# A linear-attention and feed-forward kernel: batch 1 in the nine-token layout, and the first part of q as fp32 by SyncE

## The chip, the cores and the metric

One core of one Trainium2 chip. The metric is the device time of a run in microseconds (us); every figure of a run is a median of the runs named beside it. The **granted clock** is the share of its full clock that the throttle gave TensorE, as the profile records it. A profile is of one execution. Its span is about 1.7 us shorter than the device time of the same run (295.1 against 296.85 for the kernel before).

## The reference

```python
# q, k, v: (8 batches, 8 heads, 576 tokens, 64), fp32
def phi(x):
    return np.where(x > 0, x, np.exp(x) - 1.0) + 1.0
q_p, k_p = phi(q), phi(k)
kv  = np.einsum('bhsd,bhse->bhde', k_p, v)
z   = np.sum(k_p, axis=2)
num = np.einsum('bhsd,bhde->bhse', q_p, kv)
den = np.einsum('bhsd,bhd->bhs', q_p, z)[..., None] + 1e-06
x   = (num / den) -> (4608 tokens, 512)
h   = x @ w_in                                   # 512 x 2048
g   = h * (1.0 / (1.0 + np.exp(-beta * h)))      # beta: 2048 numbers
out = g @ w_out                                  # 2048 x 512
```

The kernel computes phi as min(relu(x) + 1, exp(x)), and takes beta into ScalarE's Silu and 1/beta into w_out.

## The kernel before

Batch 0 stands in a **nine-token layout**: heads 0 to 3 on partitions 0 to 63, heads 4 to 7 on partitions 64 to 127, nine tokens on each partition (64 x 9 = 576). The other batches have four tokens on each of 128 partitions and a **tail** of 64 tokens on the first 64 partitions, whose other half has to be cleared. The parts that matter here:

```python
def load_rows(dst, src, b, eng=nc.gpsimd):       # four tokens per partition, and the tail
    eng.dma_start(out=dst[:, :, 0:NJ, :]...,     in_=src[b, :, 0:MAIN, :]...)   # 128 partitions
    eng.dma_start(out=dst[0:TAIL, :, NJ, :],     in_=src[b, :, MAIN:S, :]...)   # 64 partitions

def load_nine(dst, src, h0=0, h1=HH, j0=0, j1=N9):    # nine tokens: one load for each half
    for g in range(2):
        nc.gpsimd.dma_start(out=dst[g * TAIL : (g + 1) * TAIL, h0:h1, j0:j1, :]..., in_=...)
...
small = consts.tile([P, 2], F32)
nc.vector.memset(small, 0.0)
nc.scalar.activation(small[:, 0:1], small[:, 0:1], ACTF.Exp)
nc.vector.memset(g_sb[0][:, FC - 1, :], 0.0)     # operand of the warm-up matmuls
clear_tail(1); nc.vector.memset(vraw[1][TAIL:P, :, NJ, :], 0.0)
nc.sync.dma_start(out=beta_row, in_=moe_beta.rearrange("(c p) -> c p", p=P))
load_nine(k9, k)
load_nine(q9, q, j1=4)
load_nine(v9, v, j1=6); load_nine(v9, v, j0=6); load_nine(q9, q, j0=4)
for i in range(4): ...                           # w_in, four quarters, by GpSimd
load_w_out(0); load_w_out(1); load_k(1); load_q(1)
...                                              # the front
warm(10)                                         # ten warm-up matmuls
beta_trans(); make_beta()                        # TensorE transposes beta, VectorE works on it
warm(20)                                         # twenty more
exp0(1, 0, 5); exp0(1, 5, N9); exp0(0, 0, 4)     # k first, q's first four tokens last
relu0(1, 0, 5); relu0(1, 5, N9); phi0(1, 0, 5)
relu0(0, 0, 4); phi0(1, 5, N9); phi0(0, 0, 4)
kv_mm0(kvp, 0, N9, False)                        # z
... q transposes, v's part of kv, numerator, x, feed-forward part of batch 0
load_w_out(2); load_v(1); load_w_out(3)
...                                              # batch 1's attention, inside batch 0's y matmuls
y_phase_wide(0, {
    4: [load_next(3)],
    9: [kv_mm(1), kv_evac(1), w_out_scale(3)],
    10: [q_trans(1, 0, 1), q_trans(1, 2, 3)],
    11: [num_mm(1, 0), num_norm(1, 0)], ...
```

In these traces each engine takes its instructions in the order of the program, so a matmul that waits also holds those written behind it (twenty stood behind one that waited 3.52 us in the changed kernel). Names in the profile: `xqk` and `vraw` hold the loaded q, k and v, `vaug` is v copied beside columns of ones, `qk_p` is phi(q) and phi(k), `kv_bd` the evacuated kv, `xs` a block of x, `g` the output of Silu (and at the start the buffer of q's fp32 part).

## Time and profile before

| | before |
|---|---|
| time, median of 3 runs (lowest to highest) | 296.29 us (296.06 to 296.74) |
| span of the profiled run, granted clock | 295.1 us, 1.000 |
| TensorE busy | 283.9 us, 96% |
| beta: issued, then landed after | 0.75 us, 1.5 us |
| first feed-forward matmul | 17.16 us |
| first matmul of batch 0's second product (y) | 34.16 us |
| v of batch 1 landed; its kv matmuls start | 41.84 us; 43.23 us |
| first feed-forward matmul of batch 1 | 52.53 us |

The lines behind this stand in the prediction below. In a line of the timeline the first two numbers are start and duration in us; then engine, source line, operation, output and inputs, and in brackets the idle time of the engine before it and what ended that time. Four **anchors** on TensorE are used throughout: first feed-forward matmul, first y matmul, kv matmuls of batch 1, first feed-forward matmul of batch 1.

### The profile page before, as it was taken

The page shows a single profiled execution, that of the slowest core. Times are in us where ns is not written, and L with a number is a line of the kernel's source. Part 1 is how long each engine was busy: PE and PEld are TensorE (multiplying, and loading weights), DVE is VectorE, ACT ScalarE, POOL GpSimd, SP SyncE. Part 2 cuts the span into 40 slices and gives each one's busy share as a digit, 9 for nine tenths or more (in the row PEclk, how much of TensorE's full clock was granted, in tenths as well). Part 3 has the DMA queues.
Part 4 walks back from the last instruction along what each step waited for, and adds up shares of the span by engine and source line. Part 5 has one row for each costly group of instructions (what it writes and reads, how often), then busy time and mean ns, then how long its engine had stood idle before and what let it go on. Part 6 is the DMA issues. An engine that isn't in the chain of part 4 may idle for free.

```text
span 295.1 us, 4750 instructions
## 1 busy us (share of the span) xinstructions
PE 283.9 (96%) x1891; PEld 143.9 (49%) x1912; DVE 124.0 (42%) x261; ACT 175.1 (59%) x234; POOL 52.7 (18%) x72
## 2 busy tenths in 40 slices
PE   8879999999999999999999999999999999999994
PEld 3557445644465544445444544454445444444444
DVE  4765488504365174616461646154715400110012
ACT  2788786889988780778087907790770077018500
POOL 8924474540003200330023000000000000000000
PEclk9999999999999999999999999999999999999999
DMA  7999999999637993699369945024502400120032
GB/s 103 196 207 343 256 272 192 256 193 192 89 142 100 175 131 113 130 174 154 98 129 159 159 109 124 2 71 116 127 0 72 118 36 0 38 90 16 0 73 71
DMA packets 72310, 37.09 MB, mean 126 GB/s; under 512 B 40912, under 2 KB 66784, under 8 KB 72288
## 3 DMA queue, kind: packets, MB, share of 16 engines
q0 software_dynamic: 38912, 20.45, 47.9%
q1 hardware_dynamic: 33216, 16.20, 22.9%
q8 instruction: 15, 0.25, 0.3%
q10 hardware_dynamic: 160, 0.13, 0.2%
q14 instruction: 7, 0.06, 0.1%
HBM read 36.71 MB, written 9.44 MB: 156 GB/s over the span
## 4 chain that ended last, share of the span: by engine, by line
PE 76%; DMA 9%; POOL 4%; ACT 4%; issue 4%; DVE 1%; ACTq 0%; POOLq 0%; DVEq 0%
PE mm L453 37%; PE mm L505 33%; DMA xT<-in_moe_w_out_dram 5%; DMA vraw<-in_v_dram 4%; PE att L399 3%; ACT e L229 2%; POOL xqk L131 1%; PE att L344 1%; PE mm L537 1%; POOL w_in L159 1%; ACT L229 1%; POOL vraw L131 1%; ACT g L445 1%; DVE qk_p L242 0%; POOL xqk L111 0%
## 5 line engine op out<-in xcount | busy, mean ns | idle before, releaser
L445 ACT ACTIVATE g<-mm,beta_c 128x512 bf16<-128x512 f32 (+2 forms) x156 | 97.3, 633 | 88.4 <-PE mm L453 88.1
L505 PE MATMUL mm<-w_out,g 128*128 128x512 bf16 x541 | 126.7, 379 | 1.2 <-issue 0.3
L453 PE MATMUL mm<-xT,w_in 128*128 128x512 bf16 (+2 forms) x560 | 108.1, 349 | 1.4 <-DMA w_in<-in_moe_w_in_dram 1.1
L453 PEld LDWEIGHTS <-w_in 128*128 128x128 bf16 x656 | 61.9, 98 | 62.4 <-DMA w_in<-in_moe_w_in_dram 1.2
L505 PEld LDWEIGHTS <-g 128*128 128x128 bf16 x560 | 53.0, 98 | 58.2
L515 DVE COPY y_sb<-mm 128x512 f32<-128x512 f32 x27 | 18.7, 691 | 70.6 <-PE mm L505 69.1
L229 ACT ACTIVATE e<-xqk 128x2560 bf16<-128x2560 bf16 x14 | 31.9, 2329 | 0.1
L415 DVE TENSOR_TENSOR xs<-att,rden 128x512 bf16<-128x512 f32 (+1 forms) x40 | 27.6, 689 | 1.4
L242 DVE TENSOR_TENSOR qk_p<-r,e 128x2560 bf16<-128x2560 bf16 x14 | 20.9, 1490 | 13.1 <-ACT e L229 12.4
L355 DVE CAST kv_bd<-att 64x130 bf16<-64x130 f32 x28 | 8.2, 292 | 32.2 <-PE att L344 31.8
L72 POOL DMA_DIRECT2D vraw<-in_v_dram x7 | 6.4, 909 | 84.2 <-DVE vaug L370 78.5
L413 DVE TENSOR_SCALAR den<-att 128x8 f32<-128x8 f32 (+1 forms) x40 | 6.5, 161 | 32.0 <-PE att L399 31.9
L399 PE MATMUL att<-kv_bd,q_pT 128*128 128x130 bf16 (+1 forms) x160 | 15.8, 221 | 1.1 <-DVE kv_bd L370 0.7
L399 PEld LDWEIGHTS <-q_pT 128*128 128x128 bf16 (+1 forms) x160 | 11.6, 100 | 10.7 <-DVE xs L415 2.4
L453 PE MATMUL mm<-xT_tail,w_in 128*128 128x512 bf16 x63 | 13.9, 379 | 0.1
L237 DVE TENSOR_SCALAR r<-xqk 128x2560 bf16<-128x2560 bf16 x14 | 11.6, 834 | 3.8 <-DMA xqk<-in_q_dram 2.3
L575 PE MATMUL mm<-g 128*128 128x512 bf16 x34 | 9.9, 452 | 1.2 <-DVE g L143 1.2
L229 ACT ACT_TABLE_LOAD x7 | 9.0, 1283 | 0.1
L414 DVE RECIPROCAL rden<-den 128x8 f32<-128x8 f32 (+1 forms) x40 | 8.1, 202 | 1.4
L72 POOL DMA_DIRECT2D xqk<-in_k_dram x7 | 6.9, 984 | 6.3 <-DMA w_in<-in_moe_w_in_dram 2.8
L76 POOL DMA_DIRECT2D xqk<-in_k_dram x7 | 7.4, 1057 | 1.5 <-DMA w_in<-in_moe_w_in_dram 1.3
L256 ACT ACTIVATE e<-xqk 128x1280 bf16<-128x1280 bf16 (+1 forms) x4 | 4.4, 1155 | 5.4 <-DMA xqk<-in_k_dram 5.3
(71 smaller groups left out, 140.0 us busy)
## 6 DMA issues: line engine op xcount, KB each, us to landing
out_dram<-y_sb SPq DMA_DIRECT2D x28, 256.0 KB, 2.3
xqk<-in_k_dram POOLq DMA_DIRECT2D x7, 512.0 KB, 10.7
xqk<-in_q_dram POOLq DMA_DIRECT2D x7, 512.0 KB, 11.3
vraw<-in_v_dram POOLq DMA_DIRECT2D x7, 512.0 KB, 11.3
w_in<-in_moe_w_in_dram POOLq DMA_DIRECT2D x4, 512.0 KB, 11.0
g<-in_moe_w_out_dram POOLq DMA_DIRECT2D x4, 512.0 KB, 10.9
out_dram<-y_sb SPq DMA_DIRECT2D x14, 128.0 KB, 5.2
xqk<-in_moe_w_out_dram POOLq DMA_DIRECT2D x2, 512.0 KB, 14.4
```

The source lines that it names most:

```text
L72: eng.dma_start(out=dst[:, :, 0:NJ, :].rearrange("p h j d -> p h (j d)"), in_=src[b, :, 0:MAIN, :].rearrange("h (p j) d -> p h (j d)", j=NJ),)
L229: nc.scalar.activation(st[b, "e", a][:, h0:h1], xqk[b % NX][:, a, h0:h1], ACTF.Exp)
L237: nc.vector.tensor_scalar(st[b, "r", a][:, h0:h1], xqk[b % NX][:, a, h0:h1], 0.0, 1.0, ALU.max, ALU.add)
L242: nc.vector.tensor_tensor(st[b, "p"][:, a].rearrange("p j (h d) -> p h j d", h=H)[:, h0:h1], st[b, "r", a][:, h0:h1], st[b, "e", a][:, h0: ...
L355: nc.vector.tensor_copy(kv_bd[b % 2][i][gs, :, g, :], st[b, "kvp"][gs, 2 * i : 2 * i + 2, :])
L399: nc.tensor.matmul(nps[:n, p // 2, c0 : c0 + 2 * (D + 1)], st[b, "qT"][:, t, p, :n], kv_bd[b % 2][p // 2][:, p % 2], start=True, stop=True ...
L415: nc.vector.tensor_mul(xs[:n], nv[:, :, :, 0:D], rden[:n, :, :, None].to_broadcast([n, 2, 4, D]))
L445: nc.scalar.activation(g_sb[b % 2][:, ff, c0:c1], hp[:, c0:c1], ACTF.Silu, scale=beta_c[:, ff : ff + 1],)
L453: nc.tensor.matmul(hp[:, c0:c1], w_in_sb[ff // 4][:, kc, (ff % 4) * P : (ff % 4 + 1) * P], x[:, t0:t1, kc, :] if b < B else x[:, kc, c0:c1 ...
L505: nc.tensor.matmul(yp, g_sb[b % 2][:, ff, t * P : (t + 1) * P], w_out_sb[ff // 4][:, ff % 4, :], start=(ff == 0), stop=(ff == FC - 1),)
L515: nc.vector.tensor_copy(y_sb, yp)
L575: nc.tensor.matmul(st["warm"], g_sb[0][:, FC - 1, 0:P], g_sb[0][:, FC - 1, :], start=True, stop=True, skip_group_check=True,)
```

## The change

Its intent: batch 1 takes the nine-token layout too, so that its tail loads, tail clearing and empty columns go. And the first four tokens of batch 0's q come through SyncE as fp32, while GpSimd issues the load of k, so that GpSimd's queue is shorter and idle DMA time at the start is used. The diff, cut to its core:

```diff
+    va9 = nine(vaug[1], "jhd", EA)
+    QF = 4
+    q_first = g_f[:, 0 : HH * QF * D].rearrange("p (h j d) -> p h j d", h=HH, j=QF)   # fp32
-    def load_nine(dst, src, h0=0, h1=HH, j0=0, j1=N9):
+    def load_nine(dst, src, b, j0=0, j1=N9, eng=nc.gpsimd):
 ...
-    clear_tail(1)
-    nc.vector.memset(vraw[1][TAIL:P, :, NJ, :], 0.0)
+    load_nine(q_first, q, 0, 0, QF, eng=nc.sync)
     nc.sync.dma_start(out=beta_row, in_=moe_beta.rearrange("(c p) -> c p", p=P))
-    load_nine(k9, k)
-    load_nine(q9, q, j1=4)
+    load_nine(x9[0][1], k, 0)
 ...
-    load_k(1)
-    load_q(1)
+    load_nine(x9[1][1], k, 1)
+    load_nine(x9[1][0], q, 1)
 ...                                   # the front: q's first part ahead of k
-    exp0(1, 0, 5) ... phi0(0, 0, 4)
+    exp9(0, 0, 0, QF); relu9(0, 0, 0, QF); phi9(0, 0, 0, QF)
+    exp9(0, 1, 0, 5); exp9(0, 1, 5, N9); relu9(0, 1, 0, 5); relu9(0, 1, 5, N9)
+    phi9(0, 1, 0, 5); phi9(0, 1, 5, N9)
 ...
-    load_v(1)
+    load_nine(v9[1], v, 1)
 ...                                   # batch 1
-    phi(1, 1); v_copy(1); phi(1, 0)
+    phi9(1, 1); v_copy9(); phi9(1, 0); tidy(1)        # tidy clears the tails for batch 4 and 3
+    def kv1():   36 matmuls of 130 columns, evacuation, ones for the later batches
+    def q1():    32 small transposes into one pair of banks, three copies by ScalarE
-        9: [F(kv_mm, 1), F(kv_evac, 1), F(w_out_scale, 3)],
-        10: [F(q_trans, 1, 0, 1, wide=True), F(q_trans, 1, 2, 3, wide=True)],
+        9: [F(kv1), F(w_out_scale, 3)],
+        10: [F(q1)],
```

Batch 1's rows of the output are stored as eight stores of 64 rows, not four of 128.

## The prediction

> **What bounds the kernel now.** I read the page first (busy shares, then the forty slices), then the chain of waits, then the waits of TensorE, then the timeline of the two stages that the change touches, and last the DMA's table in half-microsecond windows.
>
> ```profile
> PE 283.9 (96%) x1891; PEld 143.9 (49%) x1912; DVE 124.0 (42%) x261; ACT 175.1 (59%) x234; POOL 52.7 (18%) x72
> PE   8879999999999999999999999999999999999994
> DMA  7999999999637993699369945024502400120032
> PE 76%; DMA 9%; POOL 4%; ACT 4%; issue 4%; DVE 1%; ACTq 0%; POOLq 0%; DVEq 0%
> ```
>
> TensorE is busy 283.9 of 295.1 us, so everything that is not TensorE work comes to 11.2 us. The chain gives 76% to matmuls; its DMA and POOL pieces all lie before 42 us. The page's row of slices shows no hole after the third slice. A change that leaves the 541 + 560 large matmuls alone can only win from those 11.2 us, and from the small matmuls of batch 1. The first 1.2 us and the last 3 us are not touched.
>
> ```profile
> PE mm L453 <- DMA w_in<-in_moe_w_in_dram: 1.1, 1, 1.1
> PE att L399 <- DVE kv_bd L370: 0.7, 1, 0.7
> PE mm L433 <- DVE xs L415: 0.4, 1, 0.4
> PE mm L453 <- ACT xT L372: 0.3, 1, 0.3
> PE att L282 <- DVE qk_p L270: 0.3, 1, 0.3
> PE att L380 <- DVE kv_bd L355: 0.3, 1, 0.3
> PE att L344 <- DVE vaug L370: 0.3, 1, 0.3
> ```
>
> These are TensorE's waits up to 60 us. The first matmul of the feed-forward part waits 1.1 us for the first quarter of w_in. The waits on kv_bd (0.7), xs (0.4) and qk_p (0.3) belong to batch 0's attention; those on vaug and kv_bd (0.3 each, the last two lines) to batch 1's. The front, from the timeline:
>
> ```profile
> 7.49 3.16 ACT L256 ACTIVATE e<-xqk 128x1280 bf16<-128x1280 bf16 x3 [5.25 <-DMA xqk<-in_k_dram]
> 10.06 1.31 DVE L270 TENSOR_TENSOR qk_p<-r,e 128x1024 bf16<-128x1024 bf16 x2
> 11.68 1.19 PE L307 MATMUL mm<-vraw,qk_p 64*128 64x128 bf16 x36
> 15.88 0.42 DVE L370 COPY xT<-mm 128x512 bf16<-128x512 bf16 x1 [0.16 <-PE mm L433]
> 17.16 1.07 PE L453 MATMUL mm<-xT,w_in 128*128 128x128 bf16 x16 [1.10 <-DMA w_in<-in_moe_w_in_dram]
> ```
>
> k lands at 7.49, all of phi is ready at 11.37, the first block of x at 16.30, but w_in only at 17.1: the load ends last here, by 0.8 us. Batch 1's stage:
>
> ```profile
> 41.91 1.27 DVE L370 COPY vaug<-vraw 128x2560 bf16<-128x2560 bf16 x1 [0.69 <-DMA vraw<-in_v_dram]
> 43.10 1.47 DVE L242 TENSOR_TENSOR qk_p<-r,e 128x2560 bf16<-128x2560 bf16 x1
> 43.23 0.82 PE L344 MATMUL att<-vaug,qk_p 128*64 128x65 bf16 x40 [0.28 <-DVE vaug L370]
> 45.51 1.94 ACT L372 ACTIVATE q_pT<-att 128x1024 bf16<-128x1024 bf16 x2 [2.49 <-PE att L380]
> 40.00:50.00 10.00, 9.15 (x101) 5.25 (x101) 8.72 (x17) 6.14 (x8) 4.97 (x7) 1.00 1.44 243
> ```
>
> v lands at 41.84, VectorE copies it, then makes phi(q) and evacuates kv_bd, and TensorE (9.15 of 10 us busy) loses 0.85 us. VectorE at 8.72 of 10 is nearly full there.
>
> The DMA windows: columns after the five engines are clock, DMA share and GB/s, counted as bytes written, so a cast from fp32 reads twice that.
>
> ```profile
> 1.50:2.00 0.50, 0.50 (x2) 0.15 (x1) 0.50 (x2) 0.50 (x1) 0.50 (x2) 1.00 0.07 17
> 2.50:3.00 0.50, 0.50 (x3) 0.22 (x2) 0.50 (x2) 0.00 (x0) 0.50 (x2) 1.00 0.77 58
> 3.50:4.00 0.50, 0.50 (x3) 0.15 (x1) 0.28 (x4) 0.00 (x0) 0.50 (x2) 1.00 1.20 198
> ```
>
> From 3 us on the DMA is full: some 190 GB/s written, 380 read. Only before 2.5 us it is idle, but for beta's 8 KB, which SyncE issued at 0.75 and which moved before 2.0.
>
> **What the Trainium skill says.** "DMA: Bandwidth & Descriptors", section "Issuing engines are not separate DMA queues": loads issued by SyncE and by GpSimd run on the same 16 engines. So the new q load adds no bandwidth; it can win only what was idle. The trace agrees in that the total stays at one level, 180 to 210 GB/s written, from 3.5 to 22 us, however many loads are open. Same page, "SWDGE vs HWDGE vs iDMA": a cast in the load needs GpSimd. That is why this part of q comes as fp32. No run here shows the refusal. "TensorEngine Tiling (Array Packing)", section "Key Properties": row tiles work independently, and a change of tiling drains. The trace agrees on the first: 36 matmuls of 64 rows and 128 columns, 217 ns each, took 1.19 us, 33 ns from one to the next. "VectorE: DVE Perf Modes", section "Mode 2×_2P": an fp32 tensor_scalar can still make two results a cycle. The w_out scaling, 512 fp32 to bf16 in 0.48 us, is quicker than 512 cycles at the page's 0.96 GHz (0.53 us), so it agrees.
>
> **The change, part by part.**
>
> Start of the loads. 512 KB of q go out on SyncE at about 0.75 us, instead of 2 x 128 KB written by GpSimd behind k. By the beta load they move from about 1.6 us. At some 390 GB/s they need 1.35 us, of which 0.9 us lie before 2.5, in idle time; the other 0.45 us share with k. All GpSimd loads after k are also issued 1.26 us sooner (the two issues at 2.59 go). As the DMA is full, the landing of w_in moves by the idle time that was filled: 17.1 - 0.9 = 16.2 us. k loses the 0.45 us to the new load but no longer has q's pieces behind it; I expect it at 7.2 to 7.5, as before.
>
> Front arithmetic. VectorE starts on q after beta's small operations, which end at 7.03 as before (TensorE's ten warm-up matmuls gate them). Then: relu of 1024 fp32, estimated 0.75 (0.62 in bf16); phi(q) 0.68; two relus of k 1.15; phi(k) 0.83 + 0.68; together 4.1, gaps 0.15, so ready at 11.3, against 11.37 now. VectorE is the limit, not ScalarE, so doing q early wins nearly nothing here. But now k's phi comes last and not q's: behind it TensorE still has 16 z matmuls (about 0.25 us), then the 16 transposes and v's 36. End of these: 11.3 + 0.25 + 0.24 + 1.19 = 13.0, now 12.87. The rest of the front is unchanged: x ready at 16.4 instead of 16.3. With w_in at 16.2 the first matmul starts at 16.4, not 17.16: -0.75. The second block of x needs VectorE's second normalisation, ready at 17.34 now and 17.45 then; TensorE takes it up at 18.07 now, about 17.5 then. So I count 0.55 us from the front.
>
> Batch 1's loads. Each tensor now has two DMAs of 256 pieces of 2,304 B in place of 1,024 pieces of 1,024 B plus 512 of 256 B. From the landings (k, q and their tails end at 36.2, the w_out part before them at 29.9) a tensor of 1.18 MB takes 3.15 us; at 2,304 B I estimate the 400 GB/s at which w_in and w_out run, 2.9 us. Three tensors save 0.8 us. v then lands at 41.84 - 0.9 - 0.8 = 40.1. Its wait goes.
>
> Batch 1's arithmetic. exp, relu, phi and the copy of v run over 2,304 instead of 2,560 elements: a tenth less, that is 0.45 of 4.57 us on ScalarE, some 0.25 of 2.9 on VectorE for both phis. Then the 0.75 us of clearing tails (0.48 + 0.27) moves from the idle start into the full stretch of VectorE, ahead of the kv_bd evacuation. The kv matmuls become 36 of 130 columns in place of 40 of 65: 36 x 33 ns = 1.2 us against 0.82: +0.35. The q transposes become 32 + 4 small ones: at the 0.41 us of 16 in the front about 0.75 + 0.2, against 1.24 + 0.29: -0.55. The waits on vaug and on kv_bd go: -0.55. But the transposed q is now copied in three pieces, 0.6 + 0.6 + 1.02 us on ScalarE in place of 1.94, all from one pair of banks, and the second numerator needs that pair: I give back 0.3 us there, and 0.1 for mode changes. Net about -0.35, rounded down to -0.3 because VectorE is so full.
>
> Sum: -0.55 - 0.3 = -0.85 us. 296.29 - 0.85 = 295.4 us. The stores of batch 1 are eight of 64 rows in place of four of 128, far from the end: nothing.
>
> **The rivals.** First, the front takes all of it back: w_in early, but x late. For it speaks that VectorE has no slack between 7.03 and 11.4 and that k's matmuls now follow the last phi; if the fp32 load delays k by 0.8 us or more, or beta behind it lands after 5.6 us, x comes at 17.1 and the front gives nothing: 295.9 to 296.5. Against it: k's load no longer shares with the old q. Second, batch 1's stage turns from waiting for v to waiting for VectorE (tails and kv_bd) or for ScalarE's three copies: then its 0.3 is lost, and some 0.2 more: 295.7 to 296.0. The slice with 8.72 of 10 speaks for it; that the inputs are ready 1.7 us sooner speaks against it. Third, all waits go at once: front 0.8, batch 1 0.85 of idle time and 0.2 in matmuls: 294.4. The stretch from 65 to 83 us, where ScalarE's exponentials lead the chain, starts from TensorE's own results, so it should move along and neither eat nor add.
>
> **Range and chances.** The front may give 0 to 0.8, batch 1 from -0.2 to 1.0; the three runs of before spread over 0.7 us. I take 294.4 to 296.5 for 8 in 10. 2% is 5.9 us, more than half of all the time in which TensorE does not work, and no part of the change comes near it: faster 0.01, slower 0.01, within 0.98.
>
> **What would show it.** Right: the first feed-forward matmul at 16.2 to 16.7 with no wait, or a short one, on w_in; phi(k) last at 11.2 to 11.5; v landed near 40; no wait on vaug; kv matmuls of 1.1 to 1.3 us; small q transposes under 1 us in all; from 100 us on, the same timeline shifted by 0.5 to 1.2 us. Wrong: k after 8.2; TensorE waiting for beta; a new wait of over 0.4 us on the copies of transposed q or on kv_bd; or a shift that is there at 60 us and gone at 100.

## The result, and the profile after

The changed kernel takes 301.14 us (median of 4 runs, 300.49 to 301.47), the kernel before 296.43 in the same comparison (4 runs). The ratio is 1.0157, 95% interval 1.0135 to 1.0179. A ratio is always the mean time of one kernel's runs over that of the other's of the same rounds, so it is not quite the ratio of the medians. The kernel became 4.7 us slower: under 2%, but far outside the predicted range of 294.4 to 296.5, and in the other direction.

The page of the changed kernel (busy shares, two rows of the forty slices, the chain's shares):

```profile
PE 286.3 (96%) x1903; PEld 144.6 (48%) x1924; DVE 122.9 (41%) x262; ACT 174.8 (58%) x234; POOL 49.5 (17%) x70
PE   5889999999989999999999999999999999999994
PEclk9599999999999999999999999999999999999998
PE 86%; ACT 5%; issue 3%; DVE 2%; DMA 2%; SPq 0%; ACTq 0%
```

The span grew by 4.6 us (295.1 to 299.7), but TensorE is busy 2.4 us longer, with only twelve instructions more. The reason stands in the third line: in the second slice, from 7.5 to 15 us, the granted clock is 0.5. The first slice of TensorE fell from 8 to 5 tenths. So both new idle time and slower work lie in the first 15 us. DMA's share of the chain fell from 9% to 2%: the loads that led before no longer lead, because TensorE is later than they are. The start of that chain, in start and duration:

```profile
2.23 6.35 DMA beta_row<-in_moe_beta_dram
8.72 0.26 PE mm L191
8.97 7.32 PE mm L611 x20
16.29 0.54 PE mm L323 x36
```

Beta's 8 KB, issued at 2.23, needed 6.35 us. TensorE's transpose of beta (L191) waited for it, the twenty warm-up matmuls (L611) stand behind that in TensorE's order and took 7.3 us, and only then comes z (L323). It is the longest of TensorE's waits up to 60 us, and no wait on vaug or w_in is among them any more:

```profile
PE mm L191 <- DMA beta_row<-in_moe_beta_dram: 3.5, 1, 3.5
```

The busy times of the engines in two windows of the front (PE, PEld, DVE, ACT, POOL; then clock, DMA share, GB/s):

```profile
5.00:8.00 3.00, 0.19 (x1) 0.00 (x0) 0.00 (x0) 0.66 (x1) 2.91 (x5) 1.00 1.24 215
8.00:14.50 6.50, 5.78 (x15) 2.19 (x16) 4.84 (x11) 2.61 (x3) 5.23 (x7) 0.50 1.34 200
```

From 5.19 to 8.72 TensorE is idle. From 8.0 to 14.5 (14.8 in finer windows) it runs at half its clock. Beta costs VectorE the same idle time: its first beta operation waits 6.31 us for the transpose, though q has lain there since 7.3. The timeline of the front:

```profile
7.34 1.06 ACT L264 ACTIVATE e<-g 128x1024 bf16<-128x1024 f32 x1 [5.10 <-DMA g<-in_q_dram]
9.01 0.17 DVE L197 COPY beta_s<-mm 128x16 f32<-128x16 f32 x1 [6.31 <-PE mm L191]
10.21 0.88 DVE L272 TENSOR_SCALAR r<-g 128x1024 bf16<-128x1024 f32 x1
21.39 1.05 PE L487 MATMUL mm<-xT,w_in 128*128 128x128 bf16 x16 [0.29 <-DVE xT L404]
```

The first anchor moved from 17.16 to 21.39: +4.23 us. The second moved from 34.16 to 38.56, +4.40. Batch 1's stage:

```profile
44.77 0.97 DVE L358 COPY vaug<-vraw 128x2304 bf16<-128x2304 bf16 x1
47.29 1.21 PE L338 MATMUL att<-vaug,qk_p 64*128 64x130 bf16 x36
49.40 0.64 PE L291 MATMUL att<-identity,qk_p 64*128 64x64 bf16 x32
50.08 2.00 ACT L406 ACTIVATE q_pT<-att 128x512 bf16<-128x512 bf16 x3 [3.09 <-PE att L291]
57.01 0.60 PE L487 MATMUL mm<-xT,w_in 128*128 128x256 bf16 x4
```

No wait stands in front of the kv matmuls, yet the last anchor moved by 4.48 us (52.53 to 57.01). So the stage takes 18.45 us from the second anchor, not 18.37: its expected gain of 0.3 is absent. One more thing looks harmless here and is not: v landed at about 43.4, later than the 41.84 of before, though everything ahead of it was meant to be quicker. It costs nothing only because TensorE came 4.4 us late.

From this I formed **theory 1**: beta's late landing is the whole cause, by idle time, half clock and the order of TensorE and VectorE. The rivals lie in batch 1: its arithmetic got slower, or its loads, which each cover 64 partitions, land late (called theory 3 in the later expectations). Under the rivals, taking the wait for beta away would leave the time high.

### The profile page after: what moved, and what is told of

Its sections match the earlier page's. It is cut to its first block, busy times and chain, and to the rows that moved or that the text cites. A ratio compares the mean times of both kernels' runs of the same rounds, so it can differ in the third digit from the quotient of the medians.

```text
span 299.7 us, 4785 instructions
## 1 busy us (share of the span) xinstructions
PE 286.3 (96%) x1903; PEld 144.6 (48%) x1924; DVE 122.9 (41%) x262; ACT 174.8 (58%) x234; POOL 49.5 (17%) x70
## 4 chain that ended last, share of the span: by engine, by line
PE 86%; ACT 5%; issue 3%; DVE 2%; DMA 2%; SPq 0%; ACTq 0%
PE mm L487 39%; PE mm L541 35%; PE att L433 3%; PE mm L611 2%; DMA beta_row<-in_moe_beta_dram 2%; ACT e L227 1%; PE att L378 1%; PE mm L573 1%; PE att L487 1%; ACT g L479 1%; ACT L227 1%; PE mm L467 1%; DVE w_out L210 1%; PE mm L323 1%; DVE kv_bd L404 0%
## 5 line engine op out<-in xcount | busy, mean ns | idle before, releaser
L541 PEld LDWEIGHTS <-g 128*128 128x128 bf16 x560 | 52.9, 98 | 58.5 <-issue 0.3
L551 DVE COPY y_sb<-mm 128x512 f32<-128x512 f32 x27 | 18.7, 691 | 70.5 <-PE mm L541 68.4
L227 ACT ACTIVATE e<-xqk 128x2560 bf16<-128x2560 bf16 x12 | 27.4, 2329 | 0.1
L240 DVE TENSOR_TENSOR qk_p<-r,e 128x2560 bf16<-128x2560 bf16 x12 | 17.9, 1492 | 13.1 <-ACT e L227 12.4
L389 DVE CAST kv_bd<-att 64x130 bf16<-64x130 f32 x24 | 7.0, 292 | 32.1 <-PE att L378 31.8
L72 POOL DMA_DIRECT2D vraw<-in_v_dram x6 | 5.3, 883 | 86.7 <-DVE vaug L404 80.7
L611 PE MATMUL mm<-g 128*128 128x512 bf16 x34 | 12.4, 539 | 1.2 <-DVE g L143 1.2
L406 ACT ACTIVATE q_pT<-att 128x512 bf16<-128x512 bf16 (+2 forms) x8 | 4.9, 661 | 9.1 <-PE att L291 9.1
L235 DVE TENSOR_SCALAR r<-xqk 128x2560 bf16<-128x2560 bf16 x12 | 9.7, 816 | 0.0
L611 PEld LDWEIGHTS <-g 128*128 128x128 bf16 x35 | 4.3, 130 | 8.1 <-issue 6.0
L72 POOL DMA_DIRECT2D xqk<-in_q_dram x6 | 7.1, 1182 | 5.7 <-ACT g L479 2.3
L264 ACT ACTIVATE e<-xqk 128x1280 bf16<-128x1280 bf16 (+2 forms) x5 | 7.6, 1562 | 0.5 <-DMA xqk<-in_k_dram 0.5
```

The costliest lines, as they stand in the source:

```text
L72: eng.dma_start(out=dst[:, :, 0:NJ, :].rearrange("p h j d -> p h (j d)"), in_=src[b, :, 0:MAIN, :].rearrange("h (p j) d -> p h (j d)", j=NJ),)
L227: nc.scalar.activation(st[b, "e", a][:, h0:h1], xqk[b % NX][:, a, h0:h1], ACTF.Exp)
L235: nc.vector.tensor_scalar(st[b, "r", a][:, h0:h1], xqk[b % NX][:, a, h0:h1], 0.0, 1.0, ALU.max, ALU.add)
L240: nc.vector.tensor_tensor(st[b, "p"][:, a].rearrange("p j (h d) -> p h j d", h=H)[:, h0:h1], st[b, "r", a][:, h0:h1], st[b, "e", a][:, h0: ...
L541: nc.tensor.matmul(yp, g_sb[b % 2][:, ff, t * P : (t + 1) * P], w_out_sb[ff // 4][:, ff % 4, :], start=(ff == 0), stop=(ff == FC - 1),)
L551: nc.vector.tensor_copy(y_sb, yp)
```

## The experiments

All outputs are right. Where an edit is said to be made in another experiment's kernel, that one's edit is kept. All ratios are to the kernel before in the same rounds.

### The wait for beta

**beta_first**: beta's load goes out on SyncE ahead of q's.

```diff
-    load_nine(q_first, q, 0, 0, QF, eng=nc.sync)
     nc.sync.dma_start(out=beta_row, ...)
+    load_nine(q_first, q, 0, 0, QF, eng=nc.sync)
```

> The changed kernel with one thing swapped: beta's 8 KB go out on SyncE ahead of the first part of q, not behind it. Theory 1 (the loss is beta: it lands at 8.6 us, TensorE stands 3.5 us before the beta transpose, its clock falls, and the twenty warm-up matmuls and VectorE's queue are late behind it): beta lands before 3 us, no wait on beta, granted clock 1.0 throughout, first feed-forward matmul at 16.5 to 17.2 us, time 295.8 to 296.8, equal to before. Rival (the fp32 load of q, sharing the DMA engines with k, delays the front by itself, or batch 1's new layout costs time): beta no longer waits, but the time stays above 299.

Measured: 300.21 us (4 runs, 299.84 to 300.65), ratio 1.0125 (1.0109 to 1.0142). Theory 1's number was missed. TensorE no longer waits for beta, which is transposed at 5.61, but it waits 2.55 us for phi instead:

```profile
9.45 1.06 ACT L264 ACTIVATE e<-g 128x1024 bf16<-128x1024 f32 x1 [7.21 <-DMA g<-in_q_dram]
12.94 0.43 PE L323 MATMUL mm<-ones,qk_p 64*128 64x2 bf16 x20 [2.55 <-DVE qk_p L278]
```

q was issued at 1.22 and not at 0.75, 0.47 us later, and was there at 9.45 and not at 7.34, 2.1 us later. At the end of this wait the granted clock fell too: it was 0.50 from 12.8 to 19.7 us. The first anchor stands at 20.50. This run moved the delay, it did not remove it.

**beta_act_queue**: beta goes through ScalarE's queue, so that neither load waits for the other's issue.

```diff
-    nc.sync.dma_start(out=beta_row, ...)
+    nc.scalar.dma_start(out=beta_row, ...)
```

> The changed kernel with beta issued by ScalarE, behind its first table load, so at about 2.2 us as in the changed kernel, but on another queue. If beta was late because it stood behind q's pieces in SyncE's queue: it lands within about 3 us of its issue, by 5.5, TensorE waits under 0.3 us for it, time 295.8 to 297. If it was late because all sixteen engines were full with k and q: it lands near 8 us again and the time is 300 to 301.5.

Measured: 300.55 us (4 runs, 299.52 to 302.0), ratio 1.0145 (1.0112 to 1.0177). The edit was meant to issue beta as late as in the changed kernel, but it went out at 0.92 us and landed 1.6 us later. So it repaired the front and left open why beta had been late. The front is now on time: q at 7.29, phi ready at 11.61, the first anchor at 16.58, though k comes at 8.66. The time hardly moved, and the timeline of batch 1's stage shows why:

```profile
44.66 0.76 DVE L358 COPY vaug<-vraw 128x2304 bf16<-128x2304 bf16 x1 [0.82 <-DMA vraw<-in_v_dram]
45.48 1.21 PE L338 MATMUL att<-vaug,qk_p 64*128 64x130 bf16 x36 [2.92 <-DVE vaug L358]
```

v comes at 44.6, and TensorE, on time now, waits 2.92 us for it. Theory 1 falls as the whole cause. There is a second fault, which the first one hid (theory 2 in the later expectations: v of batch 1 lands late).

**beta_behind_phi**: beta stays late on SyncE, but its transpose and VectorE's five operations on it stand behind phi, and 24 warm-up matmuls run without a break.

```diff
-    beta_trans(); make_beta(); warm(20)
+    warm(24)
 ...  exp9, relu9, phi9 of the front
+    beta_trans(); make_beta()
```

> The changed kernel with beta as late as there, but the beta transpose and VectorE's five small beta operations moved behind the last phi, and 24 warm-ups in one go. Theory 1 says that not the late landing costs time but what stands behind it in two in-order queues: the first feed-forward matmul then comes at 16.5 to 17.5, time 295.8 to 297. If a late k or q is what costs: phi of k still ends near 14 us and the time stays above 299.

Measured: 300.51 us (299.36 to 301.35), ratio 1.0137 (1.0104 to 1.0171). The first anchor stands at 16.76, so beta's landing at 8.6 does no harm where nothing stands behind it. The end did not move with it: v again holds TensorE, by 1.77 us in the profiled run.

**warm12**: the changed kernel with twelve warm-up matmuls behind beta, not twenty.

```diff
-    warm(20)
+    warm(12)
```

> The changed kernel with 12 instead of 20 warm-ups behind the beta transpose. There the twenty end at 16.2 us while phi is ready at 14.1, because 14 of them run at half clock. If the warm-ups stand in the way: the twelve end near 14.1, the first feed-forward matmul comes up to 2.1 us sooner (19.3 instead of 21.4), time 299.0 to 299.8. If only VectorE's late phi counts: no change, 300.5 to 301.5. If the clock is not back by then: slow matmuls after 14 us and a time of 300 or more.

Measured: 299.56 us (299.0 to 300.25), ratio 1.0109 (1.009 to 1.0127), 1.6 us under the changed kernel, as expected.

```profile
8.85 4.43 PE L611 MATMUL mm<-g 128*128 128x512 bf16 x12
13.50 0.40 PE L323 MATMUL mm<-ones,qk_p 64*128 64x2 bf16 x20 [0.22 <-DVE qk_p L278]
```

The twelve end at 13.3, 369 ns each, and z waits a moment for phi. So in the changed kernel the warm-up matmuls themselves, at 7.39 us for twenty against 4.49 before, stood in the way by 2.1 us (they ended at 16.2, phi at 14.08).

**old1_beta_late**: the new front with beta behind q on SyncE as in the changed kernel, but batch 1 in its old layout. It is old_batch1, shown below, with one line turned back:

```diff
-    nc.scalar.dma_start(out=beta_row, ...)
+    nc.sync.dma_start(out=beta_row, ...)
```

> old_batch1 (296.1) with beta back behind q on SyncE, as in the change: the first fault alone, without batch 1's new layout. Beta lands near 8.6, TensorE waits 3 to 3.6 us for it, the first feed-forward matmul comes at 21.0 to 21.6, v no longer waits for anything. If the two faults hide each other: each costs over 4 us alone, so 300 to 301 here, and together (the change) only 301.1. If they add up instead: the late beta costs only what the change costs beyond nine_only, so under 297.

Measured: 299.24 us (4 runs, 299.19 to 300.69), ratio 1.0101 (1.008 to 1.0121), a little under what was expected. Against old_batch1's ratio of 0.9991 the late beta alone costs 1.1%, some 3.2 us. The profile shows the 3.52 us of waiting and the first anchor at 21.45.

**beta_act_late**: is beta late because it stands behind q on one queue, or because the engines are full by 2.3 us? Here, in old_batch1, ScalarE writes one column of beta's buffer first, which holds the load back until then:

```diff
+    nc.scalar.activation(beta_row[:, 0:1], small[0:FC, 0:1], ACTF.Copy)
     nc.scalar.dma_start(out=beta_row, ...)
```

> The kernel old_batch1 (q first by SyncE, beta by ScalarE's own queue, batch 1 in the old layout), but ScalarE writes one column of beta_row first, so the load of beta can only be issued at about 2.3 us, as late as in the changed kernel, and on a queue on which nothing stands before it. If beta was late in the changed kernel because it stood behind the two q loads on SyncE's queue, it lands here within some 2 us of its issue, before 5 us, and nothing else moves (296 to 297). If it was late because the DMA engines were full by 2.3 us, it lands at about 8 us again, TensorE waits 2.5 to 3.5 us for it, and the time is near that of old1_beta_late, 298.5 to 300.

Measured: 299.74 us (2 runs, 299.11 and 300.37), ratio 1.0102 (1.0047 to 1.0157). Beta's tile in this kernel:

```profile
L149 ACTq DMA_DIRECT2D beta_row<-in_moe_beta_dram x1: 400/400/400, 2.5 to 2.5; - x1
DMA to landing us min/median/max: 6.1/6.1/6.1
```

Issued at 2.5 us on a queue with nothing ahead of it, it still takes 6.1 us, and TensorE waits 3.04. So the queue's order is not needed to make it late. Being issued after the large loads is enough.

**before_sp_late**: the kernel before, with the same holding line ahead of its own beta load on SyncE, and no q on that queue.

> The kernel before, with the same one-column write ahead of beta's load on SyncE's queue, so beta goes out at about 2.3 us with no q ahead of it on that queue; k and q by GpSimd are open by then, but have not begun to move much. If a queue's own order was the cause, beta lands within 2 us and the time stays at 296 to 297. If full engines were the cause, it depends on how full they are at 2.3 us, which is less than in the changed kernel: it lands somewhere from 4 to 7 us.

Measured: 297.07 us (2 runs, 296.41 and 297.74), ratio 1.0012 (0.9955 to 1.007). Beta, issued at 2.5, takes 4.4 us; TensorE waits 2.15 us for it, and the first anchor stands at 18.48. With k alone ahead of it, and not the 512 KB of q, the load is 1.7 us quicker than in beta_act_late, and still three times slower than the 1.5 us of its early issue.

### The second fault

**old_batch1**: the new front with beta by ScalarE's queue, and batch 1 as in the kernel before (loads, tails, matmuls, stores).

```diff
+    clear_tail(1); nc.vector.memset(vraw[1][TAIL:P, :, NJ, :], 0.0)
-    nc.sync.dma_start(out=beta_row, ...)
+    nc.scalar.dma_start(out=beta_row, ...)
-    load_nine(x9[1][1], k, 1); load_nine(x9[1][0], q, 1)
+    load_k(1); load_q(1)
 ...  -load_nine(v9[1], v, 1) +load_v(1), and batch 1's stage as before
```

> The first half of the change alone, without its fault: q's first part by SyncE, beta on ScalarE's queue, batch 1 in the layout of before. Theory 2, formed after the first four runs (the front is fine once beta is early, the first feed-forward matmul comes at 16.6; what costs then is v of batch 1, which lands at 44.5 instead of 41.8): v lands at 40 to 42, TensorE waits under 1 us on vaug, time 295.2 to 296.2, a little under before. Rival (the new front fills the DMA engines so that v lands late in any layout): v near 44, wait on vaug of 2 to 3 us, time 299 to 301.

Measured: 296.10 us (6 runs, 295.69 to 296.61), before 296.48 (8 runs), ratio 0.9991 (0.9977 to 1.0005); span 294.4. The first anchor stands at 16.53, v lands in time (copied at 41.61), the kv matmuls start at 42.49 without a wait, batch 1's feed-forward part at 51.95:

```profile
42.49 0.82 PE L380 MATMUL att<-vaug,qk_p 128*64 128x65 bf16 x40
```

It is the best version, though its interval holds 1.

**nine_only**: the reverse: the front of the kernel before (q through GpSimd, beta alone on SyncE), batch 1 in the nine-token layout. The edit is the change's second half.

> The second half alone: front of before (k, then q, both by GpSimd, beta alone on SyncE), batch 1 in the nine-token layout. Theory 2: v lands at 43.5 to 45.5, TensorE waits 1 to 3 us on vaug and the stage of batch 1 grows by another 1 us of VectorE work that is now in line behind v; time 298.5 to 300.5. Rival (batch 1's layout is harmless): 295.8 to 296.8 and v by 42.

Measured: 300.85 us (4 runs, 300.44 to 302.78), ratio 1.0166 (1.0126 to 1.0206). The first anchor is where it was (17.18), v is copied at 44.88, TensorE waits 2.72 us for it:

```profile
45.70 2.13 PE L336 MATMUL att<-vaug,qk_p 64*128 64x130 bf16 x36 [2.72 <-DVE vaug L356]
```

These 36 matmuls took 2.13 us, not 1.21, because the granted clock fell to 0.50 at the end of the wait, for 3.4 us. The new layout of batch 1 alone costs as much as the whole change (the verdict is unclear, since the interval passes 2%). The bytes written up to 33 us are the same as before, within some 30 KB. At 41 us this kernel is 100 KB behind and at 42 us 160 KB.

**probe**: six loads more at the end of GpSimd's program in the kernel before, results unused, each waiting for the one before it, when no other load from HBM is left: twice (a) 590 KB (fp32) to 64 partitions, (b) the same bytes to 128 partitions, (c) 1.05 MB to 128 partitions in pieces of 1,024 B.

> The kernel before with six loads at its end, each waiting for the one before it, results unused: twice (a) 590 KB read into 64 partitions in pieces of 2,304 B, (b) the same bytes and pieces into 128 partitions, (c) 1.05 MB in pieces of 1,024 B into 128 partitions. If a load into 64 partitions uses only half of the DMA engines: (a) takes clearly longer than (b), by 1 us or more (590 KB at half of 390 GB/s is 3.0 us, at the full rate 1.5), and as long as (c) with nearly twice the bytes. If the number of partitions is of no account: (a) and (b) within 0.3 us of each other, (c) 1.2 us longer. The time of the whole kernel tells nothing.

Measured (one look, 297.76 us, state unknown; each figure is the time from one issue to the next, which waits for the landing, and (c) could be read once): (a) 4.57 and 5.98 us, (b) 5.43 and 6.81, (c) 6.10. A load to 64 partitions was not slower than the same bytes to 128 in either round. But the loads ran from 208 to 243 us and were not alone: SyncE's stores and DMA transposes moved 2.56 MB in that time beside their 2.23, and not evenly. So this speaks against the guess that such a load uses half of the DMA engines, and does not settle it.

**half_parts** and **half_heads**: the kernel before, its layout and arithmetic untouched; only the three large loads of batch 1 are cut in two. One cut gives each load 64 partitions and all heads, the other gives each 128 partitions and half the heads. Bytes, piece size and number of loads are the same.

```diff
+        if b == 1:
+            for i in range(2):
+                cut = slice(i * TAIL, (i + 1) * TAIL)                    # half_parts
+                cut = (slice(None), slice(i * HH, (i + 1) * HH))         # half_heads
+                eng.dma_start(out=to[cut], in_=fr[cut])
```

> The kernel before with each of batch 1's three large loads (128 partitions, 1,024 B pieces) cut into two of 64 partitions each. Theory 3: v later than in before by 1.5 us or more (43.3 or later), TensorE waits 1 to 2.5 us longer on vaug, time 297.5 to 299.5. Rival (not the partitions): as half_heads.

> The control to half_parts: the same three loads cut into two by heads, each still writing all 128 partitions; as many loads, same pieces, same bytes. Theory 3: v within 0.7 us of before (41.2 to 42.5), time 296 to 297. Rival (more and smaller loads through eight slots make v late): as late as half_parts, both 1 us or more later than before.

Measured: half_parts 299.4 us (4 runs, 298.12 to 302.42), ratio 1.012 (1.0076 to 1.0163); half_heads 296.66 (296.09 to 297.0), ratio 1.0011 (0.9997 to 1.0024). The timeline of half_parts (its profiled run is the slowest of its four):

```profile
45.59 0.83 DVE L374 COPY vaug<-vraw 128x2560 bf16<-128x2560 bf16 x1 [0.75 <-DMA vraw<-in_v_dram]
46.47 1.31 PE L348 MATMUL att<-vaug,qk_p 128*64 128x65 bf16 x40 [3.15 <-DVE vaug L374]
```

and of half_heads:

```profile
41.61 0.83 DVE L374 COPY vaug<-vraw 128x2560 bf16<-128x2560 bf16 x1 [0.89 <-DMA vraw<-in_v_dram]
42.59 0.82 PE L348 MATMUL att<-vaug,qk_p 128*64 128x65 bf16 x40
```

Four microseconds lie between the two copies of v, and the two kernels differ only in which partitions a load covers. v's large loads, with the time from issue to landing last, in half_parts and then in half_heads:

```profile
vraw<-in_v_dram POOLq DMA_DIRECT2D x2, 256.0 KB, 10.7
vraw<-in_v_dram POOLq DMA_DIRECT2D x2, 256.0 KB, 8.4
```

The first of them was also issued later, at 33.26 us against 31.14, because before many of its issues GpSimd waits for an earlier load to land. This shows the outcome that theory 3 forecast: in this full queue, loads of 64 partitions land late, whatever the layout computes. The reason that the theory gives, queues that fall behind, is not shown. Part of the time comes through the clock: in half_parts' profiled run it was 0.50 for 6.8 us, from the wait on. But its two runs with a mean granted clock of 1.0 took 298.12 and 299.07 us, still above all four of half_heads.

**tidy_late**: a share of the blame was still open for the clearing of tails ahead of the kv evacuation. In beta_act_queue it moves to the end of the stage.

```diff
-    tidy(1)
-        14: [F(num_mm, 1, 3), F(num_norm, 1, 3), F(q1_tail)],
+        14: [F(num_mm, 1, 3), F(num_norm, 1, 3), F(q1_tail), F(tidy, 1)],
```

> The kernel of beta_act_queue with the 0.75 us of tail clearing moved from in front of the kv_bd evacuation to the end of the stage. There the stage from the kv matmuls (45.48) to the last four feed-forward matmuls (67.82) grew by 1.4 us over before, and I blame VectorE, which has the v copy, phi of q, the clearing, kv_bd and w_out's scaling in one line behind v. If so: 0.5 to 0.8 us less than beta_act_queue, 299.7 to 300.1, v as late as there. If VectorE's line is not what counts: no change, 300.3 to 300.8.

Measured: 299.87 us (298.32 to 301.12), ratio 1.0103 (1.0069 to 1.0138), within the scatter of beta_act_queue. v still lands late (wait 3.03 us). The part of the stage behind the kv matmuls is 0.24 us shorter, although the granted clock was 0.50 for 3.4 us of it and stayed at 1.0 in beta_act_queue's profile. So the clearing may cost more than 0.24; the times (0.7 us apart by the medians) can't tell.

### Attempts at a version that keeps the layout

The loads can be regrouped: even heads on partitions 0 to 63, odd heads on 64 to 127, so that one load of two heads for each half covers all 128 partitions. Only the order of the heads in xs has to be turned back.

```diff
-        for g in range(2):
+        s = src[b].rearrange("(h g) (p j) d -> (g p) h j d", g=2, j=N9)
+        for i in range(2):
+            hs = slice(i * HH // 2, (i + 1) * HH // 2)
-                out=dst[g * TAIL : (g + 1) * TAIL]..., in_=src[b, g * HH : (g + 1) * HH]...
+                out=dst[:, hs]..., in_=s[:, hs, j0:j1, :]...
```

**parity2**: this in beta_act_queue, for batches 0 and 1.

> The changed kernel with beta on ScalarE's queue, and all nine-token loads regrouped: even heads on partitions 0 to 63, odd heads on 64 to 127, so that each load writes all 128 partitions (two loads of two heads per half in place of two of 64 partitions). Same number of loads, same bytes, same pieces of 2,304 B; only the partitions that one load covers differ. Theory 3 (loads that write 64 partitions let some of the 16 queues fall behind, so loads land late though the same bytes have moved): v lands at 39.5 to 41.5, TensorE waits under 0.5 us on vaug, time 295.3 to 296.5. Rival (the size of the pieces or the order of the issues makes v late): v at 43.5 to 45 again, wait of 2 us or more, time 299.5 to 301.

Measured: 297.7 us (6 runs, 296.22 to 298.71), ratio 1.0045 (1.0023 to 1.0067). v is copied at 40.7, with no wait on it, as expected. But k lands at 9.45, the first anchor is at 17.36, and the time misses the 295.3 to 296.5 that was expected.

**parity_front**: this in nine_only, with the late clearing of tidy_late.

> nine_only (300.9) with all nine-token loads writing 128 partitions (even heads below, odd heads above) and the tail clearing moved to the end of batch 1's stage: front of before, no late beta, no late v. If only the loads were wrong in the second half of the change: v by 41, no wait on vaug, time 295.2 to 296.2, under before. If its arithmetic costs too (copies of q in three pieces, VectorE's line): 296.2 to 297.

Measured: 298.74 us (6 runs, 296.94 to 299.19), ratio 1.0064 (1.0041 to 1.0087). A miss: v is in time, but k lands at 8.37, the granted clock is 0.50 from 12.4 to 15.9 us, and the first anchor is at 18.16.

**parity0**: the kernel before, with only batch 0's loads regrouped.

> The kernel before with nothing but batch 0's loads regrouped so that each writes 128 partitions; batch 1 in its old layout, q by GpSimd, beta first on SyncE. If loads of 64 partitions hold up what follows them: w_in lands 0.5 to 1 us sooner (by 16.6), TensorE's wait on w_in goes, time 295.2 to 296.0. If the front is bound by bytes alone: 296.2 to 296.7.

Measured: 297.18 us (6 runs, 296.32 to 299.8), ratio 1.0036 (1.0003 to 1.0068). Another miss. In the profiled run, the slowest, w_in lands at 18.7 with a wait of 2.77 us. For batch 0 the regrouped loads do not help, and the times scatter over 3.5 us. The clock makes part of the scatter: in the profiled run it was 0.50 for 6.8 us, from this wait on, and the three runs with a mean granted clock below 0.995 took 297.52 to 299.8 us, the other three 296.32 to 296.84. Why w_in is late in some runs is open.

**parity1**: so batch 1's loads alone are regrouped, in beta_act_queue, with the late clearing.

> The changed kernel with beta on ScalarE's queue, batch 1's three nine-token loads regrouped to write 128 partitions each (batch 0's as in the change), tail clearing at the end of the stage. Front as in old_batch1: first feed-forward matmul at 16.4 to 16.8. If my -0.3 us for the stage was right: v by 41, no wait on vaug, time 295.6 to 296.0, under old_batch1's 296.1. If the stage's arithmetic costs: 296.2 to 297, with waits on xs or on the q copies in the profile. If the first load of k is late here too, or v is late: over 297.5, and the layout of the loads is not understood.

Measured: 297.0 us (5 runs, 296.63 to 297.04), before 296.44, ratio 1.0018 (1.0005 to 1.0032). The first anchor is at 16.70, v is copied at 40.91, the kv matmuls start at 42.56 without a wait. Both faults are gone. The kernel is still 0.18% above the kernel before, with an interval that does not hold 1, and 0.9 us above old_batch1 by the medians. From the second anchor to the last it takes 18.24 us (33.84 to 52.08), where old_batch1 takes 18.29 (33.66 to 51.95).

## Why the prediction was wrong, point by point

**The cause.** The change has two faults, and the runs show each alone. Late beta costs some 3.2 us (old1_beta_late against old_batch1). Batch 1's new layout costs some 4.5 to 5 (nine_only 1.66%; beta_act_queue 1.0145 against old_batch1 0.9991). Its loads of 64 partitions are the larger part: 2.7 us in half_parts against half_heads, and 2.9 by the medians between tidy_late and parity1, which differ in batch 1's loads and the order of its heads. The rest is shown only as a sum: 0.7 us from beta_act_queue to tidy_late, within the noise, and 0.9 from parity1 to old_batch1. Together the two faults cost 4.7 and not 8, because a TensorE that is 4.4 us late no longer has to wait for a v that is late. That is also why repairing the front alone (beta_act_queue, beta_behind_phi) gained under one microsecond: the wait for v took its place. In several runs a wait of over 2 us cost twice, once as idle time and once through the halved clock that came with it.

**Start of the loads.** The prediction saw that "8 KB" of beta stood behind 512 KB of q and named "beta behind it lands after 5.6 us" as a sign of its first rival, but gave that rival 295.9 to 296.5 with "x comes at 17.1". The mechanism was named and the term was mis-sized. The step that failed is that VectorE starts on q after "beta's small operations, which end at 7.03 as before": they ended at 10.29, since beta landed at 8.58 and not in time for the end of the ten warm-up matmuls. Behind it stood, in TensorE's order, twenty warm-up matmuls, which ran at half clock (7.39 us, not 4.49), and in VectorE's order all of phi. x came at 21.3. Its own sign of failure, "TensorE waiting for beta", carried no number. beta_act_late shows that the late issue behind the large loads is enough; it needs no q ahead on the same queue.

The idle time that q was to fill was misread too. The prediction has q's bytes move "from about 1.6 us", with 0.9 us of them before 2.5. In the changed kernel the DMA moved nothing before 2.25 us and some 20 KB from there to 2.5. w_in came early all the same: GpSimd's issue that waits for its first quarter went out at 15.63 us, against 17.41 before. So no wait on w_in was forecast rightly, but partly by luck, as the idle time before 2.5 us did not give it. The level of "180 to 210 GB/s written, from 3.5 to 22 us" has a gap as well: 126 GB/s from 6 to 7 us.

The Trainium skill, "TensorE: Matmul & The Clock Gate", section "What's actually happening", has a rule that would have warned of this: after an idle window of some 3.4 us the array's clock halves. The trace agrees in kind: TensorE stopped at 5.19, and from 8.0 on, 2.8 us later, the granted clock was 0.50. It stayed there for 6.8 us, but only for 3.4 in warm12, after a wait of 3.10, so part of this cost varies from run to run.

**k at "7.2 to 7.5".** It landed at 8.85 (8.66 with beta out of the way): a step that failed by 1.2 to 1.6 us. Its load no longer shares with q's old pieces, as argued, but shares with 512 KB that were issued half a microsecond sooner. "k after 8.2" was a sign of being wrong that the prediction named, and it came. In the repaired front this cost little, since VectorE had q to work on meanwhile.

**Front arithmetic.** Right once beta is early: first feed-forward matmul predicted at 16.4, measured 16.53 to 16.76 in five kernels, and no wait on w_in, as predicted. The fp32 relu was put at 0.75 us and took 0.69 to 1.09. The 0.55 us that the prediction drew from this are of the right size: old_batch1's anchors stay 0.5 to 0.6 us early up to 205 us, and its span is 0.7 shorter. Of that the timed runs show 0.3.

**Batch 1's loads.** "at 2,304 B I estimate the 400 GB/s at which w_in and w_out run", hence v "at 40.1". This is the step that failed for the second fault. v came at 44.6 with a front in time. The estimate looked at the size of the pieces and not at the partitions that one load covers. The Trainium skill advises against such a pair of loads: "DMA: Bandwidth & Descriptors", section "Rules for kernel authors", says of two transfers to disjoint partition halves that they serialize, and "Use one 128-partition transfer". half_parts against the kernel before, which has one such transfer, agrees with the advice (299.4 against 296.32 us). half_heads shows that two loads of 128 partitions do no harm (296.66). What makes such loads late is not shown by any run here.

**Batch 1's arithmetic.** Its terms were close: kv matmuls 1.21 us (predicted 1.2), small transposes 0.64 and 0.23 (0.75 and 0.2), copies of q 2.00. The sum was not. With loads in time (parity1) the stage gains 0.05 us against the old layout, not 0.3. A wait on xs is longer, 0.48 us against 0.28 in old_batch1. That the second numerator also waits for ScalarE's copies out of the one pair of banks is likely and not shown. The second rival, that the 0.3 goes into new waits, fits this stage.

**The chances.** The text said that 2% is out of reach of any part, because "no part of the change comes near it", and gave each side 0.01. Within 2% was right, partly by luck: added up, the two faults would come to some 2.6%. And the bound of 11.2 us of time outside TensorE's work limits only what can be won. It says nothing about what can be lost, and the upper end of the range, 296.5, was set as though it did.

**Still open**: what makes loads of 64 partitions late in a full queue; why loads land late in some runs when batch 0's are regrouped to 128 partitions (parity0); what the clearing of tails costs; and where the 0.9 us between parity1 and old_batch1 lie, since their last anchors are only 0.13 us apart.

## What to carry to other kernels

Before moving a large load ahead of a small one, ask what stands behind the small one in the order of each engine: here 8 KB that were issued 1.5 us later held twenty matmuls, halved the clock and cost 3 us. Issue such loads before any large one, or put their users behind work that does not need them. When a layout splits the partitions, check what each load covers, and test that alone, as half_parts does, before writing the arithmetic. And when a repair of a clear wait gains nothing, read the next anchor down the timeline: a second wait may have been hidden behind the first.

## What the Trainium skill lacked or had wrong

- "TensorE: Matmul & The Clock Gate", section "What's actually happening", gives windows of some 3.4 us both for the halving of the clock and for its return. For the return this fits: the half-clock stretches here last 3.4 us (warm12, before_sp_late, nine_only, parity_front) or twice that (6.8 in the changed kernel, beta_first and half_parts). For the halving it does not: the clock also halved after a wait of 2.15 us (before_sp_late), and at 12.4 us in parity_front with no single wait over 0.53 us in the 3.4 us before, while a wait of 2.92 us left it at 1.0 (beta_act_queue).
- "DMA: Bandwidth & Descriptors", section "SWDGE vs HWDGE vs iDMA", says that each DMA engine goes round robin between its internal queues. One would take from it that a small load on a queue of its own slips in quickly. beta_act_late's 8 KB, alone on ScalarE's queue but issued at 2.5 us behind 512 KB by SyncE and k by GpSimd, took 6.1 us; 1.6 us when issued at 0.92 (beta_act_queue). No page says how long a small load takes that is issued behind large ones.
- No page gives the cost of loads to half of the partitions in a queue that is full of other loads: here 10.7 us to landing against 8.4 for the same bytes cut by heads, and 2.7 us of the kernel's time (half_parts against half_heads).
- No page has the sensitivity of the first loads to their order: q issued 0.47 us later landed 2.1 us later (beta_first).
